# Reordering the first loads and the first residue's statistics in a fused spectral filter and token MLP kernel

## The chip, the cores and the metric

The kernel runs on one core of one Trainium2 chip. The metric is device time in microseconds, the median of several executions. The profile adds one more execution, which the hardware profiler recorded instruction by instruction.

## What is computed

```python
def reference(A_x, A_w_r, A_w_i, B_x, B_w1, B_b1, B_w2, B_b2, gate_w):
    # x: (1, 2048, 512); w1: (2048, 1792); w2: (1792, 2048); all bf16
    g = sigmoid((x * gate_w).sum(-1, keepdims=True))
    a = irfft2(rfft2(x) * (w_r + 1j * w_i))            # a global filter
    h = layernorm(x, axis=-1)                          # no scale, no shift
    u = gelu(einsum("bsd,sf->bdf", h, w1) + b1)        # MLP over the tokens
    b = (einsum("bdf,fs->bds", u, w2) + b2).transpose(0, 2, 1)
    return g * a + (1 - g) * b                         # both branches read the same x
```

## The kernel before

**Tiling.** The 2048 tokens are cut as 512q + 4a + r: a quarter q (0 to 3), a partition a (0 to 127) and a residue r (0 to 3). A block (r, q) is 128 tokens by 512 features, 128 KB, and has the number j = 4q + r. So residue 0 holds the blocks 0, 4, 8 and 12, which are (0,0), (0,1), (0,2) and (0,3). The matrix w1 is cut in the same way; its first 768 columns (six of fourteen tiles of 128) go to the buffer `wa`, one part per block, 192 KB each for residue 0.

**Stages.** For each block the layer norm needs a mean and a variance. On VectorE this is `stat` (L482 and L483); for the blocks in `ASTAT` it is two passes on ScalarE, a sum (`asum`, L492) and a sum of squares (`asq`, L496). Then ScalarE takes an inverse square root (`sq`, L486, column `rstd`), and VectorE writes the normed block into `h` (`nh`, L513) or ScalarE does (L543). TensorE multiplies each block with six tiles of w1 (`m1`, L710), six accumulators in PSUM growing in turn over the blocks 0, 8, 4, 12, 1, 5, 9, 13 and so on. Between them it runs the first step of the Fourier transform: for a residue, VectorE forms sums and differences of the four quarters (`q4s` L555, `q4a` L550, `q4b` L560 and L561), TensorE turns them with the table `ta` (`fa`, L572 to L575, four groups of four matmuls), and ScalarE copies each group from PSUM (L578). Only two PSUM buffers serve those groups. Later stages are the rest of w1, the transform along the features, the filter, the inverse, the second matrix (L1103), and a fold and store of the output.

**What sets the order.** `Plan` is a list scheduler that runs while the kernel is built. Each task has an engine, an assumed duration, a priority (lower goes first), and what it reads and writes. The scheduler models the engines and the DMA and issues the ready task with the lowest priority; the result is a fixed order for each engine. On the chip, an engine executes its order strictly, so an instruction that waits holds all that stand behind it. Changing an assumed duration or a factor of the DMA model therefore computes nothing differently, but can move instructions all through the kernel.

**Queues.** `ld_x0(q, eng, prio)` loads a block of residue 0, `ld_w10` a part of w1 for it, and `ld_ta` the table. SyncE (SP) and ScalarE (ACT) each own a hardware queue; an issue takes the issuing engine about 0.4 us. There are eight completion lanes for these two queues together: the ninth DMA waits until the first has landed, and so on. `hold` makes GpSimd wait for a block of x before it issues a later table.

**Start.** The nine matmuls of `warm` (L359) run first on TensorE. `presq` (L364) is a tiny activation that makes ScalarE load its function table.

Of the kernel before, what the change touches and what calls it, by code (L numbers as in the profile page):

```python
# [134 lines left out]
class Plan:  # L135
# [32 lines left out]
    def order(self):  # L168
        for n, t in enumerate(self.tasks):
            t.left = len(t.deps)  # L170
            for d in t.deps:
                d.users.append(t)
        caps = dict(self.caps)
        pending = {}
        key = {t: (t.prio, n) for n, t in enumerate(self.tasks)}
        for t in self.tasks:
            if not t.left:
                pending.setdefault(t.eng, []).append(t)
        clock = {}
        dma_free = pool_free = 0.0  # L180
        lanes = []
        events = [(0.0, 0, None)]
        seq = 1
        out = []
        n_done = 0
        while events:
            now = events[0][0]
            while events and events[0][0] <= now + 1e-9:
                _, _, t = heapq.heappop(events)
                if isinstance(t, Task):  # L190
                    n_done += 1
                    for f in t.free:
                        caps[f] += 1
                    for u in t.users:
                        u.left -= 1
                        lat = self.SAME.get(u.eng, 0.0) if u.eng == t.eng else self.LAT
                        u.ready = max(u.ready, now + lat)
                        if not u.left:
                            pending.setdefault(u.eng, []).append(u)
                            heapq.heappush(events, (u.ready, seq, None))  # L200
                            seq += 1
            progress = True
            while progress:
                progress = False
                for eng, ts in pending.items():
                    if clock.get(eng, 0.0) > now + 1e-9:
                        continue
                    best = None
                    for t in ts:
                        if t.ready <= now + 1e-9 and all(caps[a] >= t.alloc.count(a) for a in t.alloc):  # L210
                            if best is None or key[t] < key[best]:
                                best = t
                    if best is None:
                        continue
                    ts.remove(best)
                    for a in best.alloc:
                        caps[a] -= 1
                    out.append((now, len(out), best))
                    clock[eng] = now + best.dur
                    end = now + best.dur  # L220
                    if best.pk:
                        n, size = best.pk[:2]
                        k = best.pk[2] if len(best.pk) > 2 else 16
                        work = n * (0.009 + size / 27200.0)
                        issue = max(now, lanes[-8] if len(lanes) > 7 and eng != "POOL" else 0.0) + best.dur
                        dma_free = max(dma_free, issue + 0.8) + work / 16 * (1.45 if issue < 2.0 else 1.2 if issue < 6.0 else 1.0)
                        if eng == "POOL":
# [43 lines left out]
def kernel(  # L271
# [36 lines left out]
    add = pl.add  # L308
# [53 lines left out]

    def presq():
        A.activation(t["ombb2"][:, 0:1], t["eps"][:], ActF.Abs_reciprocal_sqrt, bias=t["eps"][:, 0:1], scale=1.0)  # L364
    add("ACT", 0.4, presq, reads=["eps"], writes=["omg"], prio=-8.85)


    NF = 6
# [13 lines left out]
    def ld_x0(q, eng, prio):  # L382
        ld([("x", 0, q)], lambda q=q: t["x"][:, q, 0, :], x4[:, q, 0, :], (P, 1024), prio, eng)
# [6 lines left out]
        ld([("ta", r)], lambda r=r: t["ta"][:, r, :], tabs["ta"][:, r, :], (P, 1280), prio, eng, [("hold", r - 1)] if r else [])  # L390

    ld_x0(0, "SP", -9)
    ld_x0(2, "ACT", -9)
    ld_w10(0, "SP", -8.9)
    ld_x0(1, "ACT", -8.9)
    ld_x0(3, "ACT", -8.88)
    ld_w10(2, "SP", -8.8)
    ld_w10(1, "SP", -8.7)
    ld_ta(0, -8.65)
    ld_w10(3, "SP", -8.6)  # L400
    for r in range(1, 4):
        for qs in ((slice(0, 2), slice(2, 4)) if r == 1 else (slice(0, 4),)):
# [67 lines left out]
        return t["xp"][:, 4096 + 2048 * (r % 2):6144 + 2048 * (r % 2)].rearrange("p (a c j l) -> p a c j l", a=2, c=2, j=4)  # L470

    OWN = {0: (0, 8, 4, 12), 1: (1, 5), 2: (2,), 3: (3,)}
    ASTAT = (8, 12, 5, 2)
    QS, DP = -0.2, 4.9
    sqs = []
    hk = {}
    for r in range(4):
# [10 lines left out]
        for n, j in enumerate(OWN[r]):  # L488
            pj = (-2.0, -1.95, -1.9, -1.62)[n] if r == 0 else 1.2 * r + 0.3 * n
            if j in ASTAT:  # L490
                def asum(j=j):
                    A.activation(t["gl"][:, 0:2, :].rearrange("p a d -> p (a d)").bitcast(F32), t["x"][:, j // 4, j % 4, :], ActF.Copy,  # L492
                                 scale=-1.0 / D, accum_out=t["mv"][:, j, 0:1])

                def asq(j=j):
                    A.activation(t["gl"][:, 0:2, :].rearrange("p a d -> p (a d)").bitcast(F32), t["x"][:, j // 4, j % 4, :], ActF.Square,  # L496
                                 bias=t["mv"][:, j, 0:1], scale=1.0, accum_out=t["mv"][:, j, 1:2])
                add("ACT", 0.72, asum, reads=[("x", r, j // 4)], writes=[("mvs", j), "ascr"], prio=-2 + 0.1 * n, after=[sqs[-1]] if j == 12 else ())
                aq = add("ACT", 0.76, asq, reads=[("x", r, j // 4), ("mvs", j)], writes=[("mv", j), "ascr"], prio=-2 + 0.1 * n)
            else:  # L500
                add("DVE", 0.82, lambda j=j: stat(j), reads=[("x", r, j // 4)], writes=[("mv", j)], prio=pj, after=[n0] if j == 4 else ())
            sj = add("ACT", 0.28, lambda j=j: sq(t["rstd"][:, j:j + 1], t["mv"][:, j, 1:2], 1.0 / D if j in ASTAT else 1.0),
                reads=[("mv", j), "eps"], writes=[("rstd", j)], prio=-3)

            sqs.append(sj)
            if j == 0:
                s0 = sj
            if j == 8:
                aq.deps.add(s0)

            for cs in (slice(0, D // 2), slice(D // 2, D)) if j == 0 else (slice(0, D),):
                def nh(j=j, cs=cs):
# [4 lines left out]
            if j == 0:  # L517
                n0 = nj
            if j == 8:
                n8 = nj  # L520
# [26 lines left out]
        def q4a(r=r):  # L547
            xf = t["xf", r] = t["gl"][:, 6 + 4 * (r % 2):10 + 4 * (r % 2), :]
            xs = t["x"][:, :, r, :]
            V.tensor_sub(xf[:, 2:4], xs[:, 0:2], xs[:, 2:4])  # L550

        def q4s(r=r):
            xs = t["x"][:, :, r, :]
            s = t["st"][:, 0:1024].rearrange("p (m d) -> p m d", m=2)
            V.tensor_add(s, xs[:, 0:2], xs[:, 2:4])  # L555

        def q4b(r=r):
            xf = t["xf", r]
# [1 line left out]
            V.tensor_add(xf[:, 0], s[:, 0], s[:, 1])  # L560
            V.tensor_sub(xf[:, 1], s[:, 0], s[:, 1])  # L561
        pq = -1.65 if r == 0 else 1.2 * r + 1.2 + QS
        add("DVE", tt(1024), q4s, reads=xk, writes=["st"], prio=pq, after=[n8])
        add("DVE", tt(1024), q4a, reads=xk, writes=[("xf", r % 2)], prio=pq, alloc=["xf"])
        add("DVE", 2 * tt(512), q4b, reads=["st"], writes=[("xf", r % 2)], prio=pq)

        for dq in range(4):
            def fa(r=r, dq=dq):
# [154 lines left out]
    for n, (ft, j, cs) in enumerate(order):  # L723
        last = j == jorder[-1]
        bank = "fb" if 4 <= ft < NF else "acc"
        m1t.append(add("PE", mm(cs.stop - cs.start), lambda ft=ft, j=j, cs=cs: m1(ft, j, cs),
                       reads=[("w1", w1of(ft), j)] + (hk.get(j, [("h", j)]) if cs == full else [("h", j, cs.start)]), writes=[("u", ft)],
                       prio=10 + n * 1e-3, alloc=[bank] if j == jorder[0] and not cs.start else (), free={NF - 1: ["wa"], NF + 3: ["wb"], NFT - 1: ["wb"]}.get(ft, ()) if last else ()))
        if last:
            gelus.append(add("ACT", act(512, 1), lambda ft=ft: A.activation(  # L730
                t["gl"][:, ft, :], t["u", ft][:], ActF.Gelu_apprx_tanh, bias=t["b1f"][:, ft:ft + 1], scale=1.0),
                reads=[("u", ft), "b1f"], writes=[("gl", ft)] + ([("xf", (ft - 6) // 4)] if ft >= 6 else []), prio=0.5,
                free=[bank], after=[pg]))
# [462 lines left out]
```

## Time and profile before

| | us |
|---|---|
| median of 3 runs | 124.67 (124.54 to 124.88) |
| the profiled execution, its time | 124.94 |
| its span, first to last instruction | 123.2 |
| TensorE busy | 118.0 (96% of the span) |
| VectorE busy | 113.8 (92%) |
| ScalarE busy | 84.9 (69%) |
| GpSimd busy | 42.2 (34%) |
| warm-up matmuls end, first real matmul | 5.02, 5.06 |

The profiled execution is 0.27 us longer than the median, and its time is 1.74 us more than its span. The granted TensorE clock is 1.0 in every slice. TensorE's only stops of note are those of the prediction's first view; from 12 us to its last matmul it is busy all but 1%.

### The profile page before, as it was taken

To read this page: it belongs to the slowest core of one execution; us is meant where nothing else is said; L and a number is where in the kernel's file an instruction comes from. 1 tells how busy PE (TensorE), PEld (TensorE's weight loads), DVE (VectorE), ACT (ScalarE), POOL (GpSimd) and SP (SyncE) were. 2 spreads that over 40 slices of the span, in tenths; PEclk is the share of its full clock that TensorE was granted. 3 is DMA by queue.
4 is the path that set the end of the run, shared out by engine and by line. 5 is a ranking of instruction groups with operands and counts; after the bars stand their busy time and mean duration, and the time that the engine had idled before them with its cause. 6 is when DMAs were issued, how large, how long until landed. Compare 5 with 4: busy or idle time off the path is not lost.

```text
span 123.2 us, 2197 instructions
## 1 busy us (share of the span) xinstructions
PE 118.0 (96%) x760; PEld 65.6 (53%) x774; DVE 113.8 (92%) x248; ACT 84.9 (69%) x182; POOL 42.2 (34%) x57
## 2 busy tenths in 40 slices
PE   6998999999999999999999999999999999999990
PEld 2454555546544666444455545557565566655570
DVE  1799999999999979999999999999999999999991
ACT  3869999997998699988420047238993369979500
POOL 6502428988089984889100000000000002112300
PEclk9999999999999999999999999999999999999999
DMA  3999999999999999999728800000000000214062
GB/s 95 286 366 365 366 374 195 245 351 324 340 289 197 169 284 385 397 406 343 222 39 318 340 0 3 0 0 5 3 0 5 1 0 3 118 55 176 0 255 85
DMA packets 16765, 22.80 MB, mean 185 GB/s; under 512 B 3216, under 2 KB 13858, under 8 KB 16754
## 3 DMA queue, kind: packets, MB, share of 16 engines
q1 hardware_dynamic: 15122, 19.71, 51.7%
q0 software_dynamic: 1152, 2.55, 7.5%
q10 hardware_dynamic: 480, 0.40, 1.0%
q8 instruction: 6, 0.10, 0.4%
q14 instruction: 5, 0.04, 0.1%
HBM read 20.54 MB, written 2.10 MB: 184 GB/s over the span
## 4 chain that ended last, share of the span: by engine, by line
PE 87%; DMA 7%; ACT 2%; issue 1%; DVE 0%; SPq 0%
PE acc L1103 39%; PE acc L710 30%; DMA x<-in_A_x_dram 7%; PE fb L710 4%; PE fb L669 1%; PE fa L669 1%; PE fa L574 1%; PE fa L575 1%; PE fa L572 1%; PE fa L1036 1%; PE fa L913 1%; PE fb L1037 1%; PE fa L1037 1%; PE fb L1036 1%; PE fa L899 1%
## 5 line engine op out<-in xcount | busy, mean ns | idle before, releaser
L1103 PE MATMUL acc<-gl,wb 128*128 128x512 bf16 (+1 forms) x124 | 31.3, 376 | 0.3 <-issue 0.2
L710 PE MATMUL acc<-h,wb 128*128 128x512 bf16 x124 | 29.7, 379 | 0.2
L1103 PE MATMUL acc<-gl,wa 128*128 128x512 bf16 (+1 forms) x93 | 23.5, 376 | 0.2
L1103 PEld LDWEIGHTS <-wb 128*128 128x128 bf16 x136 | 14.4, 113 | 10.6 <-issue 0.2
L710 PEld LDWEIGHTS <-wb 128*128 128x128 bf16 x128 | 12.2, 98 | 12.4
L1121 ACT ACTIVATE x<-acc,ombb,omg 128x512 bf16<-128x512 f32 x14 | 11.0, 784 | 10.0 <-PE acc L1103 7.6
L710 PE MATMUL acc<-h,wa 128*128 128x512 bf16 (+1 forms) x67 | 16.9, 371 | 0.0
L1108 POOL COPY st<-zo 128x8 bf16<-128x8 bf16 x1 | 0.4, 442 | 42.9 <-DVE zo L1061 42.9
L1103 PEld LDWEIGHTS <-wa 128*128 128x128 bf16 x102 | 10.8, 113 | 7.8
L710 PEld LDWEIGHTS <-wa 128*128 128x128 bf16 x102 | 10.0, 99 | 9.2 <-DMA wa<-in_B_w_dram 0.9
L771 POOL DMA_INDIRECT W<-in_A_w_i_dram,ix x8 | 14.1, 1766 | 1.8 <-issue 1.8
L730 ACT ACTIVATE gl<-acc,b1f 128x512 bf16<-128x512 f32 x12 | 8.3, 693 | 4.6 <-PE acc L710 4.5
L482 DVE BATCH_NORM_STATS2 stats<-x 128x6 f32<-128x512 bf16 x12 | 8.2, 680 | 2.2 <-DMA x<-in_A_x_dram 2.2
L743 ACT ACTIVATE x<-x 128x512 bf16<-128x512 bf16 x16 | 9.9, 623 | 0.0
L771 POOL DMA_INDIRECT W<-in_A_w_r_dram,ix x8 | 9.3, 1166 | 1.6 <-issue 1.3
L710 PE MATMUL fb<-h,wa 128*128 128x512 bf16 (+1 forms) x32 | 9.6, 366 | 0.1
L578 ACT CAST xp<-fa 128x512 bf16<-128x512 f32 x16 | 8.9, 578 | 1.0 <-issue 0.6
L1108 POOL COPY st<-X 128x8 bf16<-128x8 bf16 (+1 forms) x8 | 3.2, 412 | 11.7 <-ACT X L1040 8.8
L543 ACT ACTIVATE h<-x,nmr,rstd 128x512 bf16<-128x512 bf16 x8 | 6.3, 803 | 0.0
L868 ACT CAST s<-fa 8x512 bf16<-8x512 f32 x1 | 0.6, 575 | 8.2 <-PE fa L866 8.2
L669 PEld LDWEIGHTS <-X 128*128 128x128 bf16 x64 | 4.7, 98 | 2.4 <-issue 0.2
L760 POOL COPY hold<-gl 1x1 bf16<-1x1 bf16 x6 | 4.2, 695 | 4.8 <-ACT gl L730 4.8
(190 smaller groups left out, 254.2 us busy)
## 6 DMA issues: line engine op xcount, KB each, us to landing
wb<-in_B_w_dram SPq DMA_DIRECT2D x8, 512.0 KB
wb<-in_B_w_dram SPq DMA_DIRECT2D x2, 2048.0 KB
wa<-in_B_w_dram SPq DMA_DIRECT2D x1, 3072.0 KB
wa<-in_B_w_dram SPq DMA_DIRECT2D x2, 768.0 KB
out_dram<-x SPq DMA_DIRECT2D x3, 512.0 KB
x<-in_A_x_dram SPq DMA_DIRECT2D x2, 512.0 KB
wa<-in_B_w_dram SPq DMA_DIRECT2D x4, 192.0 KB
wa<-in_B_w_dram SPq DMA_DIRECT2D x2, 384.0 KB
```

Source lines behind the costliest of these rows:

```text
L482: V.bn_stats(out=t["stats"][:, j, :], in_=t["x"][:, j // 4, j % 4, :])
L543: add("ACT", act(512, 2), lambda j=j: A.activation(t["h"][:, j // 4, j % 4, :], t["x"][:, j // 4, j % 4, :], ActF.Identity, bias=t["nmr"][ ...
L578: add("ACT", act(512), lambda r=r, dq=dq: A.copy(xa(r)[:, :, :, dq, :], t["pa", r, dq][:]), reads=[("pa", r, dq)], writes=[("X", r % 2, dq ...
L669: T.matmul(pb[:, q, :, b, :], lhsT=t["X"][:, lt, e, c, 2 * b + q, :], rhs=t["tb"][:, k:k + 128], start=True, stop=True)
L710: T.matmul(t["u", ft][:, cs], lhsT=w[:, j // 4, j % 4, c * P:(c + 1) * P], rhs=t["h"][:, j // 4, j % 4, cs], start=(j == jorder[0] and not ...
L730: gelus.append(add("ACT", act(512, 1), lambda ft=ft: A.activation(t["gl"][:, ft, :], t["u", ft][:], ActF.Gelu_apprx_tanh, bias=t["b1f"][:, ...
L743: A.activation(t["x"][:, q, r, :], t["x"][:, q, r, :], ActF.Copy, accum_out=t["glog"][:, 4 * q + r:4 * q + r + 1])
L760: nc.gpsimd.tensor_copy(t["hold"][:], t["h"][0:1, n // 4, n % 4, 511:512] if kind == "h" else t["gl"][0:1, n, 0:1])
L771: add("POOL", 1.15, lambda comp=comp, lt=lt, e=e: nc.gpsimd.indirect_dma_start(out=t["W"][:, comp, lt, e, 1, 0:257], out_offset=None, in_= ...
L1103: T.matmul(t["y", j, n][:, cs], lhsT=w[:, o, 512 * q + r:512 * q + 512:4], rhs=t["gl"][:, ft, cs], start=(ft == 0), stop=(ft == NFT - 1))
L1108: nc.gpsimd.tensor_copy(s[:, :, :, 0], e[:, :, 0:129:128].rearrange("p m k -> p k m"))
L1121: A.activation(tbuf(j).rearrange("p h d -> p (h d)"), t["y", j, 0][:], ActF.Identity, bias=t["ombb2"][:, j:j + 1], scale=t["omg"][:, j:j + 1])
```

## The change

1. **Loads.** Before, ScalarE's queue issued blocks (0,2), (0,1) and (0,3) while SyncE's issued (0,0), w1's parts for q = 0, 2 and 1, the table, and after a wait w1's part for q = 3. After, SyncE's queue issues (0,0), (0,2), w1 part 0, (0,1), w1 part 2, w1 part 1, and after a wait w1 part 3; ScalarE's issues (0,3) and the table, and only after `presq`, whose priority now comes first.
2. **Statistics.** Block (0,2), j = 8, moves from ScalarE to VectorE, block (0,1), j = 4, from VectorE to ScalarE, and block (2,0), j = 2, from ScalarE to VectorE.
3. **Sums in halves.** For residue 0, `q4a` and `q4s` are split into a half that needs quarters 0 and 2, and a half that needs 1 and 3. In the built order VectorE runs the first half of `q4a` between the statistics of block 0 and its `h`, and the first half of `q4s` between the statistics of block 8 and its `h`.
4. **Planner model.** The DMA factor for issues between 2 and 6 us goes from 1.2 to 1.1, `presq` counts 1.6 us instead of 0.4, and the matmuls of block 0 count 1.6 times as long.

In the built order of TensorE the number and shapes of matmuls are the same. The first two `fa` groups stand after three matmuls of block 4 instead of five; the third stands after block 12 and two matmuls of block 1 instead of right after block 12; and the later transform stages (first matmuls of the feature transform and of the inverse) stand behind three more 512-column matmuls than before.

```diff
-                        dma_free = max(dma_free, issue + 0.8) + work / 16 * (1.45 if issue < 2.0 else 1.2 if issue < 6.0 else 1.0)
+                        dma_free = max(dma_free, issue + 0.8) + work / 16 * (1.45 if issue < 2.0 else 1.1 if issue < 6.0 else 1.0)
...
-    add("ACT", 0.4, presq, reads=["eps"], writes=["omg"], prio=-8.85)
+    add("ACT", 1.6, presq, reads=["eps"], writes=["omg"], prio=-8.95)
...
     ld_x0(0, "SP", -9)
-    ld_x0(2, "ACT", -9)
+    ld_x0(2, "SP", -8.95)
     ld_w10(0, "SP", -8.9)
-    ld_x0(1, "ACT", -8.9)
-    ld_x0(3, "ACT", -8.88)
+    ld_x0(1, "SP", -8.85)
+    ld_x0(3, "ACT", -8.9)
     ld_w10(2, "SP", -8.8)
     ld_w10(1, "SP", -8.7)
-    ld_ta(0, -8.65)
+    ld_ta(0, -8.8, "ACT")
     ld_w10(3, "SP", -8.6)
...
-    ASTAT = (8, 12, 5, 2)
+    ASTAT = (4, 12, 5)
...
-                add("DVE", 0.82, lambda j=j: stat(j), reads=[("x", r, j // 4)], writes=[("mv", j)], prio=pj, after=[n0] if j == 4 else ())
+                bj = add("DVE", 0.82, lambda j=j: stat(j), reads=[("x", r, j // 4)], writes=[("mv", j)], prio=pj, after=[n0] if j == 8 else ())
...
+            if j == 4:
+                aq.deps.add(s8)
             if j == 8:
-                aq.deps.add(s0)
+                s8 = sj
...
-        add("DVE", tt(1024), q4s, reads=xk, writes=["st"], prio=pq, after=[n8])
-        add("DVE", tt(1024), q4a, reads=xk, writes=[("xf", r % 2)], prio=pq, alloc=["xf"])
+        if r == 0:
+            for m in range(2):
+                xm = [("x", 0, m), ("x", 0, m + 2)]
+                add("DVE", tt(512), lambda q4a=q4a, m=m: q4a(m=slice(m, m + 1)), reads=xm, writes=[("xf", 0, m)], prio=pq,
+                    alloc=[] if m else ["xf"], after=[n8] if m else ())
+                add("DVE", tt(512), lambda q4s=q4s, m=m: q4s(m=slice(m, m + 1)), reads=xm, writes=[("st", m)], prio=pq,
+                    after=[n8] if m else [b8])
+        else:
+            add("DVE", tt(1024), q4s, reads=xk, writes=["st"], prio=pq)
+            add("DVE", tt(1024), q4a, reads=xk, writes=[("xf", r % 2)], prio=pq, alloc=["xf"])
...
-        m1t.append(add("PE", mm(cs.stop - cs.start), lambda ft=ft, j=j, cs=cs: m1(ft, j, cs),
+        m1t.append(add("PE", mm(cs.stop - cs.start) * (1.6 if j == jorder[0] and ft < NF else 1), lambda ft=ft, j=j, cs=cs: m1(ft, j, cs),
```

More of the change, by code (lines that the diff above doesn't have):

```diff
@@ L519 @@
             if j == 8:
-                n8 = nj
+                n8, b8 = nj, bj
         rest = [j for j in range(r, NJ, 4) if j not in OWN[r]]
@@ L545, with q4a, q4s @@
                     reads=[("x", r, j // 4), ("rstd", *g), ("nmr", *g)], writes=[("h", j)], prio=-0.5 + 0.1 * r)
-        def q4a(r=r):
+        def q4a(r=r, m=slice(0, 2)):
             xf = t["xf", r] = t["gl"][:, 6 + 4 * (r % 2):10 + 4 * (r % 2), :]
[L549 to L553, printed above, removed]
+            xs = t["x"][:, :, r, :].rearrange("p (e m) d -> p e m d", e=2)
+            V.tensor_sub(xf[:, 2:4][:, m], xs[:, 0, m], xs[:, 1, m])
+        def q4s(r=r, m=slice(0, 2)):
+            xs = t["x"][:, :, r, :].rearrange("p (e m) d -> p e m d", e=2)
             s = t["st"][:, 0:1024].rearrange("p (m d) -> p m d", m=2)
-            V.tensor_add(s, xs[:, 0:2], xs[:, 2:4])
+            V.tensor_add(s[:, m], xs[:, 0, m], xs[:, 1, m])
         def q4b(r=r):
@@ L562 @@
         pq = -1.65 if r == 0 else 1.2 * r + 1.2 + QS
-        add("DVE", tt(1024), q4s, reads=xk, writes=["st"], prio=pq, after=[n8])
-        add("DVE", tt(1024), q4a, reads=xk, writes=[("xf", r % 2)], prio=pq, alloc=["xf"])
-        add("DVE", 2 * tt(512), q4b, reads=["st"], writes=[("xf", r % 2)], prio=pq)
+        if r == 0:
[8 more added lines that the diff above has]
+            add("DVE", tt(1024), q4a, reads=xk, writes=[("xf", r % 2)], prio=pq, alloc=["xf"])
+        add("DVE", 2 * tt(512), q4b, reads=["st"] + ([(k, *e, m) for k, e in (("st", ()), ("xf", (0,))) for m in range(2)] if r == 0 else []), writes=[("xf", r % 2)], prio=pq)
         for dq in range(4):
```

## The prediction

> **What bounds the kernel now.** I read the page first, then TensorE's waits, the chain of waits up to 12 us, the start in order of time, and the DMA rate in stretches of half a microsecond.
>
> ```profile
> span 123.2 us, 2197 instructions
> ...
> PE 118.0 (96%) x760; PEld 65.6 (53%) x774; DVE 113.8 (92%) x248; ACT 84.9 (69%) x182; POOL 42.2 (34%) x57
> ```
>
> TensorE (PE) sets the time: only its idle 5.2 us can be won, and its tail after the last matmul (about 2.9 us) is not touched. The waits of PE:
>
> ```profile
> PE fa L359 <- DVE eps L324: 1.0, 1, 1.0
> PE fa L572 <- ACT xp L578: 0.4, 1, 0.4
> ```
>
> So the one stop inside the work is 0.42 us in front of the third transform group (L572). The chain of waits shows where it comes from:
>
> ```profile
> 3.92 5.30 DMA x<-in_A_x_dram
> ...
> 9.25 0.73 ACT gl L492 x2
> ...
> 10.00 0.81 ACT gl L496 x2
> 10.81 0.37 ACT rstd L486 x2
> 11.18 0.48 ACT xp L578
> ...
> 11.71 0.22 PE fa L572
> ```
>
> The first half of residue 1 is issued at 3.92 and lands at 9.22. ScalarE (ACT) has the statistics of block 5 at the head of its queue, waits for that landing, and the copy that frees the PSUM buffer stands behind. PE's start, from the order of time:
>
> ```profile
> 1.00 4.02 PE L359 MATMUL fa<-xp 128*128 128x512 bf16 x9 [1.00 <-DVE eps L324]
> 4.66 0.60 DVE L513 TENSOR_SCALAR h<-x,mv,rstd 128x256 bf16<-128x256 bf16 x2 [0.36 <-ACT rstd L486]
> 5.00 3.62 PEld L710 LDWEIGHTS <-wa 128*128 128x128 bf16 x23 [0.89 <-DMA wa<-in_B_w_dram]
> 6.03 0.40 DVE L513 TENSOR_SCALAR h<-x,mv,rstd 128x512 bf16<-128x512 bf16 x1
> ```
>
> The warm-up ends at 5.02 and real work begins at 5.06. The warm-up is unchanged, so an earlier w1 part or an earlier `h` of block 0 wins at most 0.04. Block 8's `h` is ready at 6.43, and PE takes it at 6.58 without a stop. The DMA rate (last number, GB/s):
>
> ```profile
> 2.50:3.00 0.50, 0.50 (x2) 0.15 (x1) 0.00 (x0) 0.50 (x1) 0.50 (x1) 1.00 1.20 296
> 3.00:3.50 0.50, 0.50 (x2) 0.15 (x1) 0.11 (x1) 0.49 (x2) 0.50 (x2) 1.00 1.03 191
> 3.50:4.00 0.50, 0.50 (x3) 0.19 (x2) 0.50 (x1) 0.50 (x2) 0.50 (x2) 1.00 0.85 185
> 4.00:4.50 0.50, 0.50 (x3) 0.11 (x1) 0.27 (x2) 0.50 (x3) 0.50 (x3) 1.00 0.79 239
> 5.00:5.50 0.50, 0.46 (x4) 0.38 (x4) 0.50 (x3) 0.47 (x3) 0.00 (x0) 1.00 1.07 384
> ```
>
> Summed over all stretches from 1.5 us, 131 KB (in thousands) have moved by 2.5 us, 280 by 3.0, 468 by 4.0, 587 by 4.5, 728 by 5.0, 1113 by 6.0. This is a clock for landings. Blocks (0,0) and (0,2), 262 KB, were seen to land at 3.4 to 3.55, some 0.5 after the sum passes them (2.94). With w1 part 0 and block (0,1) the sum is 590 (4.51), and they landed at 5.0 and 5.2, lag 0.5 to 0.7.
>
> **The loads.** The bytes ahead of residue 1 are the same, so I keep the clock and change the order.
> - Block (0,0) has no rival at first: 131 KB by 2.5, so it lands at 3.0 (at best) to 3.39 (as now); I take 3.1, nearer the lone transfer. Block (0,2) is second: 3.5.
> - ScalarE's table load (1.28, now at 2.15 after three issues) comes first, so block (0,3) is issued at about 2.3 instead of 1.67, and the table `ta` at 2.8 instead of 2.60.
> - w1 part 0 is then the 459th KB, or the 524th if block (0,3) takes a share: 4.5 to 4.8, hidden by the warm-up.
> - Block (0,1) is now fourth on SyncE's queue, issued near 2.1 where it was issued at 1.20. Without a share for ACT's queue it is the 590th KB and lands near 5.1; with all of (0,3) and some of `ta` in between it is the 721st to 780th: 5.0 to 5.13, plus 0.6: 5.6 to 5.75. I take 5.6, because in the old trace both queues advanced together. By the same count w1 part 2, which block 8 needs too, is the 918th to 1082nd: 6.1 to 6.6, not later than block 8's `h` below.
>
> The Trainium skill, "DMA: Bandwidth & Descriptors", section "Issuing engines are not separate DMA queues", says that issuing from several engines only saves issue time, since all share the same 16 engines. Its section "Queues, rings and completion order" has each DMA engine alternate between the queues that hold work. The trace agrees in the shared landing times above (5.0 and 5.2). By these rules one queue moves nothing faster, and the late small load on the other queue takes turns with block (0,1).
>
> **The statistics.** Block 8 on VectorE: from landing to `h` of block 0 took 4.66 - 3.39 = 1.27; the inserted half subtraction (pitch 0.34, from L560 to L561) fits the 0.36 wait for `rstd`. Then: 3.1 + 1.27 + 0.55 (4.66 to 5.21) = 4.92 start of block 8's statistics, + 0.72 + 0.22 + 0.33 = 6.19 start of its `h`, ready at 6.6: PE starts block 8 at about 6.63 against 6.58 (6.92 if block (0,0) lands as now).
> But ACT's built order puts the sum for block 4 (L492, waits for (0,1)) ahead of block 8's inverse root. Queued behind that wait are this root, the square pass, everything of block 12. From a landing at 5.6: 0.68 to the root's start (3.65 to 4.33), 0.33 to `h`, 0.40, and 0.04: PE starts block 8 at 5.6 + 1.45 = 7.05. That costs 0.47. It would cost nothing at 5.15.
>
> **The halves and block 12.** From block 8 to block 12 PE now has twelve 512-column matmuls at 0.216 and two groups (8.95 to 9.61): 3.26. So it reaches block 12 at 10.31. `h` of block 12 is now behind block 1's statistics on VectorE, which need residue 1's first half, with landing b: b + 0.82 (9.25 to 10.07) + 0.41 = b + 1.25 with a signal. The halves let the sums end at about 8.75 against 8.94, and the groups come at 9.0, so they are hidden.
> The same bytes stand ahead of b, so between 8.6 and 9.6 I take 9.1, nearest the 9.22 seen. Block 12 starts at the later of 10.31 and 10.35, and is done 1.30 later: 11.65. By then PE has done just what it had done before at 11.71. The old stop is gone: the third group now has two more matmuls ahead (0.43), and the copy follows block 5's first pass by about 2.04 (1.84, and one root of 0.20), so about 11.5, freeing the buffer by 12.1 for a group due at 12.1. Result so far: -0.06.
>
> **The rest.** VectorE gains block 2's statistics (0.82) and some 0.1 for the halves; ACT loses the two passes of block 2 (1.66). PE has three more matmuls (0.65) ahead of the inverse's first group, where VectorE finished 0.1 ahead of PE (82.19 against 82.31). VectorE also had 0.7 of waiting on ACT in between. So I price this at +0.1, with 0 to 0.3 as ends. The planner's factors act only through these orders.
>
> Sum: 124.94 - 0.06 + 0.1 = 125.0 for an execution like the profiled one. The median is 0.27 lower. Late residue 1 is what an ordinary execution may lack, and both kernels share it, so I put the same +0.04 on the median: 124.7.
>
> **The rivals.**
> - *Faster: both landings come early.* If (0,1) lands by 5.2 and b by 8.6, block 8 starts at 6.65, block 12 at 9.91 and ends at 11.21: -0.5, so 124.2. For it: the order in one queue follows the need, and the low rates at 3 to 4.5 us leave room. Against it: PE cannot start earlier, and b has the same bytes ahead.
> - *Slower: block (0,1) behind ACT's loads holds ScalarE's queue.* At 6.0 block 8 starts at 7.45 and block 12 at 10.71, done at 12.01: +0.3, with the +0.1 behind it +0.4: 125.1 from the median. If ordinary executions have no late residue 1 and so nothing for the change to remove, the same +0.4 stands on 124.94: 125.3. It decides from a landing of about 6.0 (or b of 9.5, which gives the same end). For it: fourth in one queue, sharing from 3.4 us on. Against it: 5.2 now, with as many bytes ahead.
> - *The change does not do what it says*: all queues share the engines and the landings stay. Then block 8 waits only for VectorE (6.92) and block 12 for b = 9.22 (10.47): +0.06 on the profiled execution. This lies inside the forecast's case.
>
> **Numbers.** Forecast 124.7 with 0.38 for a change within 0.3% (0.37 us, about what a measurement of this kernel can tell from no change), 0.27 for the faster rival and 0.35 for the slower one, whose wait stands in the built order, while the gain needs two landings at once. The range takes in both rivals with the ends of the small terms: 124.0 to 125.4.
>
> **What would show it.** In the profile after: PE's stop at L572 gone; a new one of about 0.4 at block 8 (near 6.6, on VectorE's `h` or w1) and a small one near 10.3 on `h` of block 12; ACT's first L492 waiting for x until 5.6. If that L492 starts before 5.2, or residue 1 lands before 8.6, the faster rival holds; if PE starts block 8 after 7.4, the slower one. A stop of PE on VectorE after 40 us would make the pricing of the later stages wrong.

## The result and the profile after

| | before | after |
|---|---|---|
| median (range), us | 124.78 (124.54 to 125.12) | 126.53 (125.80 to 128.03) |
| the profiled execution, us | 124.94 | 126.60 |
| its span, us | 123.2 | 124.8 |
| last matmul ends, us | 120.34 | 121.47 |
| last store is issued, us | 120.75 | 122.35 |

The ratio is 1.0118 with a 95% interval of 1.0084 to 1.0153: slower by 1.0 to 1.9 us. The range of after holds one slower execution (128.03), which the ratio leaves out. The forecast was 124.7 in a range of 124.0 to 125.4, so it was wrong.

The page of after, with the engines' totals and the shares of the chain that ended last:

```profile
span 124.8 us, 2213 instructions
...
PE 118.7 (95%) x774; PEld 65.4 (52%) x774; DVE 114.3 (92%) x252; ACT 83.0 (67%) x178; POOL 42.0 (34%) x57
...
PE 68%; DVE 15%; DMA 10%; issue 2%; SPq 2%; POOL 0%; DVEq 0%; POOLq 0%
```

In before the last of these lines began with PE 87%, DMA 7%, and had DVE at 0%. The chain now runs over VectorE for 15% of the span. TensorE's waits (line, what it waited for, us in total, times, longest):

```profile
PE acc L720 <- DMA wa<-in_B_w_dram: 1.3, 1, 1.3
PE fa L359 <- DVE eps L324: 1.0, 1, 1.0
PE acc L720 <- DVE h L515: 0.4, 1, 0.4
```

The old stop in front of the third transform group is gone, as predicted. Two new ones stand in its place, and both end before 8 us. VectorE's waits in after:

```profile
DVE stats L482 <- DMA x<-in_A_x_dram: 3.0, 2, 2.2
DVE xp L321 <- PEq L1190: 0.8, 1, 0.8
DVE h L515 <- ACT rstd L486: 0.6, 1, 0.6
DVE X L594 <- ACT xp L588: 0.5, 1, 0.5
DVE gl L552 <- DMA x<-in_A_x_dram: 0.4, 1, 0.4
```

They sum to 5.3. In before there were 4.1 (2.2, 0.8, 0.7 and 0.4). VectorE's busy time rose from 113.8 to 114.3. So its waits and its work grew by 1.2 + 0.5 = 1.7, close to the 1.6 by which the last store is later. The start in order of time shows where the first waits come from (start, us, engine, line, operation, and in brackets the idle time before it and what ended that):

```profile
0.74 1.28 ACT L364 ACT_TABLE_LOAD   x1 [0.74 <-PEq L1190]
...
1.00 0.40 ACTq L312 DMA_DIRECT2D x<-in_A_x_dram  x1
...
1.45 0.44 ACTq L312 DMA_DIRECT2D rot<-dft_ta  x1
...
2.13 0.43 SPq L312 DMA_DIRECT2D x<-in_A_x_dram  x1
...
4.68 0.42 DVE L552 TENSOR_TENSOR gl<-x 128x512 bf16<-128x512 bf16 x1 [0.38 <-DMA x<-in_A_x_dram]
...
5.97 0.61 PE L720 MATMUL acc<-h,wa 128*128 128x256 bf16 x4 [1.27 <-DMA wa<-in_B_w_dram]
...
6.41 0.63 ACT L492 ACTIVATE gl<-x 128x512 f32<-128x512 bf16 x1 [1.79 <-DMA x<-in_A_x_dram]
...
7.36 0.41 DVE L515 TENSOR_SCALAR h<-x,mv,rstd 128x512 bf16<-128x512 bf16 x1 [0.61 <-ACT rstd L486]
...
7.82 1.02 PE L720 MATMUL acc<-h,wa 128*128 128x512 bf16 x4 [0.37 <-DVE h L515]
```

ScalarE's queue sends block (0,3) at 1.00 and `ta` at 1.45, while its table load runs until 2.02. Block (0,2) is there at 4.68, w1 part 0 at 5.96, and block (0,1), which SyncE's queue sends at 2.13, at 6.4. ScalarE stands at the sum for (0,1) from 4.62 to 6.41 with block 8's root behind it, so block 8 starts at 7.82 (before: 6.58).

There is one more loss behind these. The row of 3.0 us above holds two waits, 2.2 at the start (as in before) and 0.80 at 15.18, where VectorE needs residue 2 of x. The chain that ended last leads there from block (0,1):

```profile
2.13 4.26 DMA x<-in_A_x_dram
...
6.41 0.42 SPq L312
...
7.39 7.76 DMA x<-in_A_x_dram
...
15.18 0.70 DVE stats L482
```

By this chain SyncE's queue sends its load at 6.41 only when block (0,1) has landed, since the loads share eight completion lanes. Residue 2 goes out at 7.39 (6.93 in before) and lands at 15.15; GpSimd's `hold`, which waits for the same load, runs at 15.27 (13.71 in before).

The end of after, in the view by time:

```profile
121.82 0.34 DVE L1161 SCALAR_TENSOR_TENSOR x<-fa,omg,x 128x128 bf16<-128x128 f32 x1
```

The last matmul and the stores are in the table. The last VectorE instruction started at 120.38 in before and starts at 121.82 now: +1.44, more than TensorE's +1.13.

### The profile page after: what moved, and what is told of

The parts are those of the page before. It is cut to its first block, busy times and chain, and to the rows that moved or that the text cites. A ratio compares the mean times of both kernels' runs of the same rounds, so it can differ in the third digit from the quotient of the medians.

```text
span 124.8 us, 2213 instructions
## 1 busy us (share of the span) xinstructions
PE 118.7 (95%) x774; PEld 65.4 (52%) x774; DVE 114.3 (92%) x252; ACT 83.0 (67%) x178; POOL 42.0 (34%) x57
## 4 chain that ended last, share of the span: by engine, by line
PE 68%; DVE 15%; DMA 10%; issue 2%; SPq 2%; POOL 0%; DVEq 0%; POOLq 0%
PE acc L720 29%; PE acc L1113 26%; DMA x<-in_A_x_dram 10%; PE fb L720 3%; DVE x L1149 3%; DVE X L1125 2%; DVE st L1122 2%; DVE st L1121 2%; DVE X L1126 2%; SPq L312 2%; PE fb L679 1%; PE fa L679 1%; PE fa L585 1%; PE fa L584 1%; PE fa L909 1%
## 5 line engine op out<-in xcount | busy, mean ns | idle before, releaser
L1113 PE MATMUL acc<-gl,wb 128*128 128x512 bf16 (+1 forms) x128 | 32.2, 376 | 0.0
L720 PE MATMUL acc<-h,wb 128*128 128x512 bf16 x128 | 30.2, 379 | 0.0
L781 POOL DMA_INDIRECT W<-in_A_w_i_dram,ix x8 | 14.9, 1858 | 1.8 <-issue 1.8
L482 DVE BATCH_NORM_STATS2 stats<-x 128x6 f32<-128x512 bf16 x13 | 8.8, 680 | 3.1 <-DMA x<-in_A_x_dram 3.0
L486 ACT ACTIVATE rstd<-mv,eps 128x1 f32<-128x1 f32 x16 | 4.6, 293 | 4.8 <-DVE mv L483 3.4
L770 POOL COPY hold<-gl 1x1 bf16<-1x1 bf16 x6 | 4.7, 786 | 4.1 <-ACT gl L740 4.0
```

Source lines behind the costliest of these rows:

```text
L482: V.bn_stats(out=t["stats"][:, j, :], in_=t["x"][:, j // 4, j % 4, :])
L486: A.activation(o, v, ActF.Abs_reciprocal_sqrt, bias=t["eps"][:, 0:1], scale=scale)
L720: T.matmul(t["u", ft][:, cs], lhsT=w[:, j // 4, j % 4, c * P:(c + 1) * P], rhs=t["h"][:, j // 4, j % 4, cs], start=(j == jorder[0] and not ...
L770: nc.gpsimd.tensor_copy(t["hold"][:], t["h"][0:1, n // 4, n % 4, 511:512] if kind == "h" else t["gl"][0:1, n, 0:1])
L781: add("POOL", 1.15, lambda comp=comp, lt=lt, e=e: nc.gpsimd.indirect_dma_start(out=t["W"][:, comp, lt, e, 1, 0:257], out_offset=None, in_= ...
L1113: T.matmul(t["y", j, n][:, cs], lhsT=w[:, o, 512 * q + r:512 * q + 512:4], rhs=t["gl"][:, ft, cs], start=(ft == 0), stop=(ft == NFT - 1))
```

## The experiments

All were timed in five rounds beside the kernel before, whose median in the batches was 124.50 to 124.81. Below, one instruction's **lag** is its start minus its start in the profiled execution of before. A single profiled execution carries some chance of its own at the start: with the same first loads, and nothing changed before 13 us, the first real weight load began at 5.00 (before) and at 5.12, 5.79, 5.08 and 5.26 in four runs below. And that execution of before (124.94) is 0.13 to 0.44 above the batches' medians, so a lag against it comes out small. So sizes are taken from the timed ratios, places from the traces.

### Parts alone, planned anew

```diff
 loads_only:    before + the new load lines and prio=-8.95 of presq
 rest_only:     after with the load lines and that prio of before
 planner_only:  before + factor 1.1, presq 1.6, first matmuls x 1.6
 stat2_only:    before + ASTAT = (8, 12, 5)        # block 2's statistics on VectorE
```

> Before, with the new load order and presq's priority alone; statistics, sums and the planner's model as before. Theory Q (the queues): ScalarE issues block (0,3) and the table at about 1.0 and 1.45, because its sequencer does not wait for the table load, so both run ahead of w1 part 0 and block (0,1); w1 part 0 lands near 5.9 instead of 5.0, so TensorE starts near 6.0 instead of 5.06 and all of it lands at the end: +0.8 to +1.6 us (125.6 to 126.4). Theory V (the extra VectorE work is what costs, loads are a side show): within 0.3 us of before. Theory P (the planner's new orders): within 0.3 us of before.

> After, with the load order and presq's priority of before; statistics, halves and the planner's factors as after. Theory Q: the early waits vanish, what is left is block (2,0)'s statistics on VectorE (0.82 us), so 0 to +0.8 us. Theory V: VectorE is saturated from 9 us to the end, so its 0.5 to 0.9 us of extra work comes out one to one: +0.5 to +0.9 us. Theory P: near all of the +1.75 us.

> Before, with the planner's factors alone (DMA 1.1, presq 1.6, block 0's matmuls 1.6). Theories Q and V: within 0.3 us of before, since the first twenty instructions of every engine stand as before. Theory P: +0.8 us or more.

> Before, with block (2,0)'s statistics alone moved from ScalarE to VectorE. Theory V: VectorE never waits after 47 us in before and its last instruction ends with TensorE's, so 0.82 us more work at 12 to 16 us comes out as +0.4 to +0.8 us at the end, unless its one later wait (0.7 us on ScalarE at 47 us) takes it up. Theory Q: within 0.3 us of before, the work is hidden as the prediction had it.

| | median, us | ratio to before (95%) |
|---|---|---|
| loads_only | 125.77 | 1.0072 (1.0043 to 1.0101) |
| rest_only | 126.15 | 1.0101 (1.0072 to 1.0131) |
| planner_only | 125.72 | 1.0072 (1.0047 to 1.0098) |
| stat2_only | 126.27 | 1.0108 (1.0075 to 1.0140) |

Each part alone costs 0.9 to 1.5 us, and the parts do not add up: loads_only and rest_only, which together are the whole change, would make 1.7% against 1.2%. Any edit makes the planner write a new order, and three of the four show a VectorE wait on ScalarE's copies that before has not. One view of VectorE's waits each, in the order rest_only, planner_only, stat2_only:

```profile
DVE X L594 <- ACT xp L588: 1.2, 1, 1.2
```

```profile
DVE X L584 <- ACT xp L578: 0.5, 1, 0.5
```

```profile
DVE X L584 <- ACT xp L578: 0.8, 1, 0.8
```

They stand at 30.3, 33.1 and 34.1 us, each behind a gate product (`x<-x,gw`) and in front of the butterflies of a residue's transform. They are not all extra: before's own wait for such a copy, 0.71 at 46 us, is in none of the four traces. By the medians, loads_only came as theory Q had it and planner_only as theory P; rest_only and stat2_only cost more than theories Q and V allowed. These four runs could not tell the queues from the new orders. The next ones hold the orders.

### The loads with all orders held

Here the planner runs on the old text, and only the first loads are put in other queues or places afterwards. Each engine's order of compute stays word for word.

```diff
     order_ = pl.order()
+    first = [...]              # the nine first loads and presq, in the order wanted
+    for p, task in zip(sorted(order_.index(k) for k in first), first):
+        order_[p] = task       # each load is emitted on the queue wanted
```

held_new_loads is the kernel before with the changed kernel's queues; held_old_loads is the changed kernel with the queues of before.

> The kernel before with every engine's order of compute held exactly as it was; only the first loads stand in the changed kernel's queues: (0,0), (0,2), w1 part 0, (0,1), parts 2, 1, 3 on SP, and the table load, (0,3) and ta on ScalarE's queue. The sums and statistics are those of before. Theory Q (the queues cost by themselves): the landings move as in the changed kernel, w1 part 0 to 5.9-6.0 and (0,1) to 6.4, the first w1 matmul starts near 5.97 instead of 5.06, VectorE is 0.8 to 1.3 us late at 10-20 us, its wait of 0.71 at 46 us takes up that much, and the end comes 0.3 to 0.7 late: 125.1 to 125.5. Theory O (the loss is made by new orders, which the new loads only set off): with the orders held the end is within 0.2 of before, 124.6 to 125.0, against 125.77 where the orders were free to follow.

> The changed kernel with every engine's order of compute held exactly as it is, and the first loads back in the queues of before ((0,2), (0,1), (0,3) on ScalarE ahead of its table load, ta on SP). Theory Q: (0,1) lands near 5.2 and w1 part 0 near 5.0 again, the start is 0.7 to 0.9 earlier, and as VectorE is the later engine from there on, 0.6 to 0.9 of the 1.75 comes back: 125.6 to 125.9. Theory O: the orders and VectorE's added work hold the loss, and the time stays at 126.2 to 126.6.

Measured: held_new_loads 125.52, ratio 1.0108 (1.0068 to 1.0147); held_old_loads 125.19, ratio 1.0047 (1.0030 to 1.0065). Theory Q got the direction of both. Its sizes were too small: 125.52 is at the top of its 125.1 to 125.5, and 125.19 is below its 125.6 to 125.9. The loads cost about 1% with no order changed. The new orders with the moved statistics and the added VectorE work cost about 0.5%; no run takes these apart. The sum, 1.55%, is just above the upper end of the 1.18% (0.84 to 1.53) of the whole change, and against held_old_loads the loads cost 0.7%. In held_new_loads the same early waits appear without any of the other parts:

```profile
PE acc L712 <- DMA wa<-in_B_w_dram: 0.9, 1, 0.9
```

```profile
DVE h L515 <- ACT rstd L488: 1.1, 1, 1.1
```

VectorE's lag is +0.62 at 11 us and +0.37 after 46 us, where it waits 0.50 for ScalarE instead of 0.71.

In held_old_loads the last matmul ends at 120.09, which is 0.25 *earlier* than in before, and yet the last store is 0.22 later (120.97): in this trace TensorE gains and VectorE's end gives it away. Set beside held_old_loads, whose orders are the same, after shows where the new loads cost time. Its block 8 starts 0.90 later. VectorE's first statistics of residue 2 start 1.72 later (15.18 against 13.46, there without a wait). From 23 us to the end TensorE and VectorE are both 1.38 later. So the late residue 2 adds about 0.5 to the 0.9 of block 8. In held_new_loads VectorE comes to residue 2 at 15.07 and does not wait.

### Which of the loads

All with held orders; w1.n is w1 part n of residue 0.

```diff
 after_late_act:           (0,3), ta stay on ScalarE's queue, behind its first rstd
 after_x2_on_scalar:       (0,2) back to the head of ScalarE's queue
 after_first_loads_on_sp:  SyncE: (0,0) (0,2) w1.0 (0,1) (0,3) w1.2 w1.1 ta w1.3; ScalarE: none
 held_first_loads_on_sp:   the same, with the orders of before
 held_four_on_scalar:      orders and queues of before, w1 part 2 as ScalarE's fourth load
 held_w1_behind_table:     the same, with w1 part 2 behind the table load
```

> The changed kernel with every order of compute held; (0,3) and ta stay on ScalarE's queue, but stand behind its first rstd (issued at about 4.5 and 5.0) where they were issued at 1.00 and 1.45. Theory A (those two early transfers are what delays w1 part 0 and (0,1)): w1 part 0 lands near 5.1 again and (0,1) near 5.6, block 8 starts near 7.05 instead of 7.82, and 0.5 to 0.9 of the loss comes back: 125.6 to 126.0. Theory S (SP's own order does it: (0,2) ahead of w1 part 0, and one queue's issues 0.43 apart): the first w1 matmul stays at 5.8-6.0 and the time at 126.2 to 126.6.

Measured: 129.87, ratio 1.0385 (1.0339 to 1.0432). Neither theory had this, but both halves of it teach something. Without the two early transfers w1 part 0 is in time for a first matmul at 4.84 (5.97 in after), (0,1) is there by 5.06 (6.41), and block 8 starts at 6.70 (7.82). Theory A was right on these landings. But (0,3), sent at 4.12, comes behind three w1 parts and half of residue 1, which SyncE's queue had sent, and lands at 10.20:

```profile
4.12 0.40 ACTq L312 DMA_DIRECT2D x<-in_A_x_dram  x1
...
10.30 0.42 DVE L554 TENSOR_TENSOR gl<-x 128x512 bf16<-128x512 bf16 x1 [3.65 <-DMA x<-in_A_x_dram]
...
11.43 0.38 PE L722 MATMUL acc<-h,wa 128*128 128x512 bf16 x1 [3.28 <-DVE h L517]
```

> The changed kernel with every order of compute held; (0,2) alone goes back to the head of ScalarE's queue, ahead of the table load, so that w1 part 0 is second and (0,1) third on SP, each 0.44 earlier; (0,3) and ta are issued behind the table load's start as in the changed kernel. Theory S: w1 part 0 lands 0.4 to 0.9 earlier (5.1 to 5.5), (0,1) near 5.9, and the end comes 0.3 to 0.6 earlier: 125.9 to 126.2. Theory A: both stay late and the time stays at 126.2 to 126.6.

Measured: 125.74, ratio 1.0103 (1.0081 to 1.0125). The landings came as theory S had them (first matmul at 5.24, ScalarE's sum for (0,1) at 6.11, block 8 at 7.51), and the last store is issued 0.80 earlier than in after. By the ratios it cannot be told from after.

> The changed kernel with every order of compute held; (0,3) and ta leave ScalarE's queue and stand in SP's: (0,0), (0,2), w1 part 0, (0,1), (0,3), parts 2 and 1, ta, part 3. Theory A (the two transfers that ScalarE's queue sent at 1.00 and 1.45 delay what stands behind them on SP): w1 part 0 and (0,1) land as where those two came late (first w1 matmul at 4.6-5.1, (0,1) at 5.1), (0,3) lands near 5.8 instead of 10.2, block 8 starts near 6.7-7.0 instead of 7.82, and the end comes 0.7 to 1.1 earlier than the changed kernel's: 125.4 to 125.8. Theory S (SP's order and pace do it): the first w1 matmul stays at 5.8-6.0 and the time at 126.2 to 126.6.

> The kernel before with every order of compute held, and the same SP order of first loads as in the run before it; ScalarE issues none and begins its table load at 0.74. Theory A: (0,0) lands 0.1 to 0.2 earlier (3.2), w1 part 0 before 5.0 and (0,1) near 5.1, so that both bounds move together by 0.1 to 0.3: 124.3 to 124.6, and the loss of the new loads (0.95 with orders held) is ScalarE's early transfers. Theory S: 125.2 to 125.6 as with the new loads.

Measured: 127.09, ratio 1.0199 (1.0172 to 1.0226), and 126.48, ratio 1.0150 (1.0124 to 1.0177). Theory A's landings came again (first matmul at 4.83, (0,1) by 4.95), and its times were 1.3 to 2.2 us too low. What came early was paid for by what came next, here in after_first_loads_on_sp:

```profile
7.39 1.04 PE L722 MATMUL acc<-h,wa 128*128 128x512 bf16 x4 [1.09 <-DMA wa<-in_B_w_dram]
...
10.35 0.69 DVE L484 BATCH_NORM_STATS2 stats<-x 128x6 f32<-128x512 bf16 x1 [2.02 <-DMA x<-in_A_x_dram]
```

w1 part 2, sent at 3.08, holds block 8, and the first half of residue 1 holds VectorE until 10.35 (9.25 in before, without a wait). The rows of stretches show that less was moved. The last two numbers are the packets' time as a share of the DMA engines' (it can pass 1) and GB/s; before first, then held_first_loads_on_sp:

```profile
2.50:5.00 2.50, 2.50 (x6) 0.60 (x4) 1.21 (x4) 2.49 (x6) 2.30 (x5) 1.00 0.94 238
5.00:7.50 2.50, 2.46 (x18) 1.79 (x18) 2.38 (x8) 1.87 (x7) 0.00 (x0) 1.00 1.10 384
```

```profile
2.50:5.00 2.50, 2.17 (x6) 0.70 (x5) 1.26 (x4) 1.32 (x4) 2.28 (x5) 1.00 0.76 222
5.00:7.50 2.50, 1.47 (x12) 1.07 (x11) 2.43 (x7) 1.95 (x7) 0.00 (x0) 1.00 0.96 298
```

The one queue sends a load every 0.47 us, and its share is 0.76 where two queues have 0.94. That the pace of issue does this is not shown: 131 to 197 thousand bytes every 0.47 us would be 279 to 418 GB/s, more than was moved. Until 4.0 us this run had even moved more than before (218 against 187 GB/s from 1.5 us on); the loss lies from 4.0 to 6.0 us (165 against 322). From 2.5 to 10 us the rate was 327 GB/s in before, 317 in held_new_loads, 300 in after and 279 here. With the orders of before, three, two and no loads on ScalarE's queue cost 0, 1.1 and 1.5%, though these runs differ in the order of the loads too. If the pace of issue were all, a fourth should help:

> The kernel before with every order of compute held and one more first load on ScalarE's queue: w1 part 2 as its fourth, ahead of the table load; SP's later loads are each one issue (0.43) earlier. Theory T (two queues that issue side by side get the first bytes in sooner; with these orders 3 loads on ScalarE's queue give the time of before, 2 behind its table load +0.95, none +1.8): 124.0 to 124.5. Rival: what sets the start is (0,0), w1 part 0 and (0,1) alone, and the table load is now 0.45 later, to 3.9, so that ScalarE's first sum (3.65) is 0.5 late: 124.7 to 125.2.

> As the run before it, but w1 part 2 stands behind the table load on ScalarE's queue, where the changed kernel's runs had such issues go out while the load ran; the table load keeps its place at 2.15. Theory T: 124.0 to 124.5. Rival (start set by the first blocks alone): 124.5 to 124.9.

Measured: 125.10, ratio 1.0042 (1.0023 to 1.0062), and 125.80, ratio 1.0100 (1.0068 to 1.0132). In the first the rival has it. The second is slower than either forecast. Both moved as much as before (260 and 382 GB/s, then 250 and 385 in the two stretches). In the first the table load starts at 2.63 instead of 2.15 and VectorE waits 0.8 on a root. In the second, part 2 goes out only at 3.35, near the end of the table load (2.15 to 3.43), and holds TensorE:

```profile
PE acc L712 <- DMA wa<-in_B_w_dram: 1.3, 1, 1.3
```

Its place in the lanes did this. In before w1 part 3 was the ninth load and waited until 3.55; here part 3 goes out at 2.60 and part 2 is the ninth, sent 0.02 after block (0,0) had landed (3.33). So this run says nothing on theory T. What these runs bear out is that the order of landings counts, and that all loads on one queue lose; why they lose stays open. No arrangement tried here was better than that of before.

### VectorE: work added and taken away

With all orders of before, one 128x1024 sum is written twice, late (the inverse's second step) or early (`q4s` of residue 1).

```diff
             V.tensor_add(dst(0, 1), p, q)
+            if inverse and stk == "st" and reads[0][1] == 0:      # extra_vector_late
+                V.tensor_add(dst(0, 1), p, q)
             V.tensor_add(s, xs[:, 0:2], xs[:, 2:4])
+            if r == 1:                                            # extra_vector_early
+                V.tensor_add(s, xs[:, 0:2], xs[:, 2:4])
```

> The kernel before with one more VectorE instruction at 81.5 us, the sum of the inverse transform's second step for frequency half 0 written a second time (128x1024, 0.68 us busy, 0.60 to the next start in the trace of before); every order is as before and nothing else is added. Theory V (VectorE is a bound of its own from 47 us to the end): every row behind it comes 0.60 later and so does the end: 125.3 to 125.5. The step of the prediction (TensorE sets the end, VectorE's extra work is hidden): 124.7 to 125.0.

> The kernel before with the same amount of VectorE work added at 17.3 us, the sum of halves of residue 1 written a second time (128x1024, 0.69 us busy, 0.60 to the next start). Theory V with the wait of 0.71 at 46.1 us as the only slack: VectorE is 0.60 late from 17 us, the wait for ScalarE's copy at 46 us shrinks to about 0.1, and the end is where it was: 124.7 to 125.0. Rival: the delay passes on to ScalarE (copies, gate sums), the wait stays, and the end is 0.6 late as with the late addition: 125.3 to 125.5.

Measured: late 125.15, ratio 1.0048 (1.0027 to 1.0068), so +0.60 us (0.34 to 0.85), all of the 0.60. Early 124.92, ratio 1.0022 (1.0006 to 1.0038), so +0.27. In its trace the lag is +0.57 behind the added sum, and the only slack of VectorE takes it up:

```profile
46.10 0.81 DVE L685 TENSOR_TENSOR B<-xp 128x512 bf16<-128x512 bf16 x2 [0.18 <-ACT xp L675]
```

The wait was 0.71 in before, at 46.11. In that trace the lag is 0 from there on; the timed median lies between the two forecasts, so ordinary executions may have a little less slack than this one. (In the trace the added sum stands at 13.1 us, not at the 17.3 of the forecast.) Now the reverse, four small instructions on GpSimd, and in the second run six more (the forecast counts seven):

```diff
     def omg():
-        V.tensor_scalar(t["omg"][:], t["g"][:], -0.5, 0.5, op0=Alu.mult, op1=Alu.add)
+        nc.gpsimd.tensor_scalar(t["omg"][:], t["g"][:], -0.5, 0.5, op0=Alu.mult, op1=Alu.add)
...
```

> The kernel before with every order held; the four small instructions that turn the gates into factors (omg, g, g's half, ombb2: 0.20, 0.21, 0.18 and 0.10 from start to start at 60.5-61.2 us on VectorE, 0.69 in all) run on GpSimd, whose last row before its end folds is at 58.85; their first reader is at 96 us. Theory V (VectorE is the bound from 47 us on): everything on VectorE behind 61 us is 0.69 earlier, and the end 0.4 to 0.69 earlier: 123.9 to 124.2. The prediction's step (TensorE sets the end): no change, 124.4 to 124.7.

> As the run before it, and the seven instructions on the edge columns (wpm, cm, ce: 63.50 to 64.31 on VectorE, 0.81) on GpSimd too; their first reader on VectorE is at 66.77. Theory V: 1.5 less on VectorE, so up to 1.5 earlier, 123.1 to 123.5, where GpSimd has ce done by then; by its rows of 0.4 each, 11 of them are 4.4 us from 60.6 on, so done at 65. If GpSimd is slower (its copies in this trace go up to 1.1), VectorE waits for ce at 65.3 and 0.8 to 2 of it is given back: 123.9 to 125.5. The prediction's step: no change, 124.4 to 124.7.

Measured: 124.74, ratio 1.0008 (0.9990 to 1.0026), and 124.52, ratio 1.0006 (0.9985 to 1.0026): no change. Theory V had the late addition right and taking away wrong. In gate_on_pool VectorE's lag goes from -0.38 (a luckier start) to -0.97 behind 61 us. Then it goes back to -0.62 at 88.8, to -0.51 at 96.7 and to -0.43 at 100.2, and is about -0.40 from there on, as TensorE's is. The first of these steps:

```profile
88.16 0.18 DVE L966 COPY X<-wt 128x4 bf16<-128x4 bf16 x1 [0.22 <-ACT wt L959]
```

VectorE has run ahead and waits for ScalarE's copies of TensorE's inverse groups. Of the 0.59 gained, nearly all is given back. In the second run the six instructions end at 66.26 on GpSimd and VectorE waits 1.14 for them (L854), as feared there.

> The run before it with the four gate factors on GpSimd as well (0.69 off VectorE at 61 us). Theory B (balance: TensorE's and VectorE's chains end together in the kernel before, so adding to either shows in full and taking from one shows nothing): what the loads give and no more, within 0.2 of the run before it. Theory V (VectorE alone is the bound): 0.4 to 0.69 less than the run before it.

> The changed kernel with the four gate factors on GpSimd (0.69 off VectorE at about 62 us), nothing else; the same edit gave 0 in the kernel before. Theory B with VectorE as the later of the two in the changed kernel (its last store is 1.60 later, its last matmul 1.13): the end comes back to where TensorE lets it, 0.4 to 0.5 earlier, 126.0 to 126.2. If TensorE sets the end here too (the step of the prediction): within 0.2 of 126.53.

Measured: 126.24, ratio 1.0124 (1.0095 to 1.0153), and 126.02, ratio 1.0117 (1.0089 to 1.0144). The first is 0.24 below its partner (126.48), at the edge of the partner's interval, so nearer to theory B (within 0.2) than to theory V (0.4 to 0.69). Its lag falls from +0.95 to +0.38 at 61 us and is +0.91 again at 100. The second does not bear out the form of B that it was meant to show: against after's 1.0118 nothing is gained, though the intervals are too wide to exclude 0.4 us. The trace is clearer. Its last store is 0.35 earlier than in after, but it was already 0.34 ahead at 46 us. The 0.59 gained at 61 came back at 87 to 97 us, as in the kernel before.

## Why the prediction was wrong

**TensorE's early path.** The rule that block 8 starts 1.45 after the landing of (0,1) and the 3.26 from there to block 12 were right: 6.41 + 1.45 = 7.86 against 7.82, and 11.08 against 11.07. The slower rival was the right mechanism, with ScalarE's queue held by (0,1) ahead of block 8's root, and its sign came (TensorE starts block 8 after 7.4). Its price, 125.1 to 125.3, was too small.

**The step that failed first: the landings.** "ScalarE's table load (1.28, now at 2.15 after three issues) comes first, so block (0,3) is issued at about 2.3 instead of 1.67, and the table `ta` at 2.8 instead of 2.60." They went out at 1.00 and 1.45, ahead of w1 part 0 (1.66) and (0,1) (2.13). With both ahead, (0,1) ends with the 885th KB (four blocks of 131, w1 part 0 with 197, `ta` with 164), which by the half-microsecond stretches of after had moved by 5.2. With the lag of 0.5 to 0.7 that the prediction read from before it is 5.7 to 5.9; it landed at 6.4, and w1 part 0 at 5.96 instead of 4.5 to 4.8. after_late_act, where the two go out later and both landings come 1.1 to 1.4 earlier, shows that they were to blame; the two runs with all first loads on SyncE's queue, where neither runs ahead, have the early landings too. The 0.5 beyond the clock stays open. The late w1 part 0 also took away the cover of the warm-up, under which it was priced at nothing. And the late (0,1) held SyncE's queue, so that residue 2 was late for VectorE by 0.80, a path that the prediction did not follow. The loads together cost 1.1% (0.7 to 1.5) with the orders of before (held_new_loads, where residue 2 held nothing) and 0.7% with the new orders (after beside held_old_loads); the sum had -0.06 us for the whole start.

**What did not fail: the clock.** The prediction took from the Trainium skill, "DMA: Bandwidth & Descriptors", section "Issuing engines are not separate DMA queues", that issuing from several engines saves issue time only, and kept the old clock. In the changed kernel, which also uses two queues, no less was moved up to 7.5 us: 276 and 362 GB/s in the two stretches, against 238 and 384 in before. Only from 7.5 to 10 us was it less (262 against 359), when SyncE's queue was already late with its loads. So the early loss is not one of bytes moved, but of whose bytes they were. The runs with all first loads on SyncE's queue did move less (222 and 298 in held_first_loads_on_sp), with a cause that no run here shows.

**The second step that failed: "+0.1" for everything later.** VectorE's added 0.9 was counted as hidden, with 0 to 0.3 as ends. held_old_loads has the later part at 0.59 us (0.37 to 0.81). The prediction noted that VectorE's work reached the inverse only 0.1 ahead of TensorE and that VectorE had 0.7 of slack. These were the right two numbers, and they say the opposite of "hidden": past that one slack, late work shows in full (extra_vector_late, +0.60). The added 0.9 stands before 20 us, where 0.60 cost 0.27 (extra_vector_early). If 0.33 of it is taken up here too, 0.57 is left; this is an estimate from that run, and it fits the 0.59. The part of the new orders in it was not taken apart, nor which entry of the planner sets the waits on ScalarE's copies at 30 to 35 us. The prediction's sign for this step, a stop of TensorE on VectorE after 40 us, did not come in after: the loss shows in VectorE's end and not as such a stop.

**What held.** That only TensorE's idle time can be won was right in its direction: 0.69 us less on VectorE won nothing. What it left out is that VectorE's chain ends together with TensorE's in the kernel before: taking 0.69 from it won nothing, and adding 0.60 late cost all of it. Nothing was added to TensorE alone. Residue 1's first half landed before its use (VectorE reached it at 9.4 without a wait), the old stop went, and the halves cost no wait of their own beyond 0.38 at 4.68.

**The sum.** Loads +1.1% and orders with VectorE's work +0.5% make 1.6%, against 1.2% (0.8 to 1.5) measured together. The difference of 0.4% lies within the intervals. Some overlap is seen in after's trace: VectorE's lag of 2.62 at 35 to 43 us fell to 1.82 where before waits 0.71 at 46 us and after does not wait.

## What to carry to other kernels

When two engines are each busy over 90%, look for where they meet before calling either one's work hidden: the idle rows of the second engine are its slack, and here there was one behind the start, of 0.71 us. For the first loads, write down for every queue when each issue will really leave, then check the order of need, and what each landing releases: here a late block also held the queue that had later loads to send. When a planner rewrites all orders on any edit, hold its orders and move one thing, or each part will seem to cost everything.

## What the runs showed of the hardware

- A DMA that stands behind a table load and a tiny activation in ScalarE's program went out while the load ran: 1.00 and 1.45, with the load from 0.74 to 2.02. In after_x2_on_scalar it was 1.27 and 1.67, with the load from 1.20 to 2.48. Behind an activation that waited for data it did not (4.12 in after_late_act, where the root ran at 4.12), nor as the ninth load of the eight lanes (3.35 in held_w1_behind_table, with the load from 2.15 to 3.43).
- After TensorE had waited 3.28 us at 8.1 to 11.4 us in after_late_act, its granted clock was 0.52 from 12.5 to 15.0:

```profile
10.00:12.50 2.50, 1.07 (x9) 0.66 (x9) 2.20 (x6) 2.22 (x6) 0.66 (x2) 1.00 1.06 387
12.50:15.00 2.50, 2.50 (x10) 1.03 (x9) 2.40 (x8) 2.29 (x9) 0.25 (x1) 0.52 1.08 363
```

- Stops of 1.27 us (after) left it at 1.00 there. So that long stop cost more than its own length. The one execution of after_late_act with a mean granted clock of 0.999 took 128.15 us; the other five, at 0.974 to 0.987, took 129.56 to 131.49.
- GpSimd needed 1.42, 1.17, 0.92 and 0.22 us for four instructions of 8 or 16 columns that take VectorE 0.17 to 0.18 each. The last of them took 1.15 in gate_and_edges_on_pool.
- With all first loads on SyncE's queue the transfers ran at 215 to 222 GB/s from 2.5 to 5.0 us and 286 to 298 from 5.0 to 7.5 (after_late_act, held_first_loads_on_sp), and at 238 and 384 in before, where two queues send.
